# More ticks behind the gate columns, one reciprocal for both halves of a tile's numerators, and the last rows scaled by two engines

## The chip, the cores and the metric

One core of a Trainium2 chip runs the whole program. The metric is device microseconds of one execution; a kernel's time is the median of its runs. Five engines have a queue each and run their queues in order: TensorE (PE; its weight loads are listed as PEld), VectorE (DVE), ScalarE (ACT), GpSimd (POOL) and SyncE (SP, which here only issues DMAs).

## The reference

Three stages follow each other. B = 2, H = 8 heads, S = 576 tokens, D = 64, 128 features.

```python
# attention with positive features
q_p, k_p = phi(q_s), phi(k_s)                       # exp(projection - max)
kv  = np.einsum('bhsm,bhsd->bhmd', k_p, v);  z = np.sum(k_p, axis=2)
num = np.einsum('bhsm,bhmd->bhsd', q_p, kv)
den = np.einsum('bhsm,bhm->bhs', q_p, z)[..., None] + 1e-06
x = num / den                                       # as 1152 x 512
# a dense block
g = (x @ w1) * (x @ w2);  x2 = (g @ w3) @ w_out     # 512 -> 1024 -> 1024 -> 512
# a mixture of 8 experts, one expert for each token
logits = x2 @ w_gate;  expert_idx = np.argmax(logits, axis=1)
h = np.maximum(np.einsum('ecd,edf->ecf', disp, w1), 0.0)
y = np.einsum('ecf,efd->ecd', h, w2)
out[i] = gate_w[i] * y[expert_idx[i], pos[i]]       # kept tokens, zero for others
```

## The kernel before, in words

Each fp32 product is made of three TensorE passes over a high and a low half of both operands (`PASS`). ScalarE casts the high half; the low half is a subtraction on GpSimd or VectorE. The weights of the dense block come as 64-bit numbers: VectorE puts three operations (L325 to L327, or L350 to L355 for later ones) to a 128x512 piece to get an fp32, ScalarE casts, GpSimd subtracts (L331, L364).

The attention phase runs over nine tiles of 128 tokens. `num(i)` makes the numerators and denominators of a tile in two halves of four heads, one PSUM bank each from a pool of two (`pm`); VectorE adds EPS to the denominators (`dn`), takes reciprocals (`rd`) and multiplies (`x`). `x_tr` transposes the result to the operands `xh`, `xl`. In the last tiles TensorE also runs products of the dense block (`ab`, w = 0 into a `pm` bank, w = 1 into another pool's) as fill. Here a scheduler orders the queues of all engines but TensorE, whose order is that of the program.

Then a string, `PLAN`, lists products: `a` is a quarter of the rows of `x @ w1` and `x @ w2` for f, `W` is a row block of w3 @ w_out, `u` and `v` are the gate columns (`gate_t` transposes the raw W, `gate_u` multiplies it by w_gate), `l` the logits. From the mark `|` on every queue has the order of the program, and the preparation of weights is a list of tasks. `tick()` gives each active task one more step, at most one step for each engine: words on VectorE (two), cast on ScalarE, low half on GpSimd. The end of a step that frees a raw buffer issues the next load on SP. `need()` ticks until a task is done.

`END` is such a string for the rest: routing, and two rounds r0 and r1 over experts. A round gathers its tokens (`f`, `F`), transposes them (`t`, `T`: `r_pt`, `r_xc`), multiplies by W (`p`, `P`: `r_x2p`, `x2h`, `x2l`), makes the hidden layer (`h`, `H`: `r_hp`) with weights e1, and the result (`s`, `S`: `r_yt`, `r_py`) with e2; `scatter` scales rows by the gate (`yo`) and GpSimd writes them to `out` by an indirect DMA, three in a round. `.` is a tick, and `1` to `4` release the tasks of a round's e1 or e2, each of four loads of 512 KB cut in two pieces of 128x512 (`r1_e1_20` is piece 0 of load 2): ScalarE casts both, VectorE makes the low half of piece 0, GpSimd of piece 1, and GpSimd's frees the raw buffer. The raw buffers are two rings of two. `x` asks for r1's e1 loads, `y` for its e2 loads. A round's pieces have the same name in the profile with the round's digit left out (`r_e_20l`).

Of the kernel before, what the change touches and what calls it, by code (L numbers as in the profile page):

```python
# [8 lines left out]
F32 = mybir.dt.float32  # L9
# [5 lines left out]
ALU = mybir.AluOpType  # L15
AX = mybir.AxisListType.X

B, H, S, D, M = 2, 8, 576, 64, 128
NT = B * S
DM = H * D  # L20
# [3 lines left out]
G = 96  # L24
BIG = 1.0e6
SCALE = float(D) ** -0.25
EPS = 1e-6 * M
# [27 lines left out]

END = "l<kAkrArfAAArfw>AAAA>AA<At.ttLttMt>1K.p..K.p..Rp..p..p..RpF.2h..h.R.h..Fh..h..h..x3h..h..s.TT.sTT.sTT.s..ssy4P..P..P..P..P..P..P.H.H.H.H.H.HHHSSSS"


@with_exitstack
def attention_moe_kernel(ctx: ExitStack, tc: tile.TileContext, qT, kT, v, om, w1, w2, w3, wo, wg, e1, e2, cap, out):
    nc = tc.nc
    V = nc.vector
    A = nc.scalar

    const = ctx.enter_context(tc.tile_pool(name="const", bufs=1))
    sm = ctx.enter_context(tc.tile_pool(name="sm", bufs=1))
# [12 lines left out]
    def px(nm):  # L81
        return psx.tile([128, 512], F32, tag="px", name=nm)

    def u(shape, dt, nm):
        return unit.tile(shape, dt, tag="u", name=nm)

    def kq(shape, dt, nm):
        return kqp.tile(shape, dt, tag="kq", name=nm)
# [7 lines left out]
    def pm(nm):  # L96
        return psm.tile([128, 512], F32, tag="pm", name=nm)
# [14 lines left out]
    late, hold, leave = [False], [False], set()  # L112
# [9 lines left out]
    def pump():  # L122
        full = set()
        for t in todo:
            r = t["ring"]
            if r and t["raw"] is None and r not in full:
                if out_of[r] < LIM[r]:
                    out_of[r] += 1
                    t["raw"] = t["load"]()
                else:  # L130
                    full.add(r)

    def tick(n=1):
        for _ in range(0 if hold[0] else n):
            used = set()
            while todo and (todo[0]["key"][0][0] != "e" or todo[0]["key"][:2] in leave) and (todo[0]["ring"] is None or sum(t["ring"] is not None for t in active) < 2):
                active.append(todo.pop(0))
            for t in list(active):
                engs, fn, end = t["st"][0]
                if used & set(engs):  # L140
                    continue
                used |= set(engs)
                t["st"].pop(0)
                fn(t)
                if end:
                    out_of[t["ring"]] -= 1
                    pump()
                if not t["st"]:
                    active.remove(t)
                    done_of[t["key"]] = t["got"].get("r", True)  # L150
# [102 lines left out]

    def num(i):
        x = tmp.tile([128, H, D], F32, tag="x", name=f"x{i}", bufs=2)
        for g in range(2):
            ps = pm(f"nu{i}_{g}")
            for h in range(4):
                hh = 4 * g + h
                for t0 in (0, 64):  # L260
                    b = 0 if i < 4 or (i == 4 and t0 == 0) else 1
                    nc.tensor.matmul(out=ps[t0:t0 + 64, h * (D + 1):(h + 1) * (D + 1)], lhsT=qpT[i][:, hh, t0:t0 + 64],
                                     rhs=kvz[b][:, hh, :], start=True, stop=True)
            p4 = ps[:, 0:4 * (D + 1)].rearrange("p (h d) -> p h d", d=D + 1)
            dn = sm.tile([128, 4, 1], F32, tag="dn", name="dn", bufs=4)
            rd = sm.tile([128, 4, 1], F32, tag="rd", name="rd", bufs=4)
            V.tensor_scalar(out=dn, in0=p4[:, :, D:D + 1], scalar1=EPS, scalar2=None, op0=ALU.add)
            V.reciprocal(out=rd, in_=dn)
            V.tensor_tensor(out=x[:, 4 * g:4 * g + 4], in0=p4[:, :, 0:D], in1=rd.to_broadcast([128, 4, D]), op=ALU.mult)
        xs[i] = x  # L270

    def x_tr(i):
# [214 lines left out]
    def gate_t(f):  # L487

        raw = raws.pop(f)
        ps = px(f"wT{f}")  # L490
        for d in range(4):
            nc.tensor.transpose(out=ps[:, d * 128:(d + 1) * 128], in_=raw[:, d * 128:(d + 1) * 128], identity=ident)
        wT[f] = kq([128, 4, 128], F32, f"wT{f}")
        A.copy(out=wT[f], in_=ps.rearrange("p (d m) -> p d m", d=4))

    def gate_u(f):
        ps = px(f"u{f}")
        t = wT.pop(f)
        for d in range(4):
            nc.tensor.matmul(out=ps[:, 0:E], lhsT=t[:, d], rhs=wgT[:, d], start=(d == 0), stop=(d == 3))  # L500
        A.copy(out=u_all[:, f], in_=ps[:, 0:E])

    def logits(f, cs):
        for c in cs:
            nc.tensor.matmul(out=lgp[c * 32:c * 32 + E, 0:C], lhsT=u_all[:, f], rhs=g_t[f][:, c * C:(c + 1) * C],
                             start=(f == 0), stop=(f == 7))
        if late[0]:
            tick()
# [18 lines left out]
    for i in range(11):  # L527
        for st in STEP:
            if st in "Tt" and i < 9:
                q_tr(i, "Tt".index(st))  # L530
            if st in "Pp":
                phi_g(11 + i, "Pp".index(st))
            if st == "N" and 1 <= i < 10:
                num(i - 1)
            if st == "X" and 2 <= i:
                x_tr(i - 2)
            if st in "Aa" and i >= 7 and fill:
                ab_mm(*fill.pop(0))
        if i == 1:
            conv12(1)  # L540
# [38 lines left out]
    for p in PLAN.split():  # L579
# [10 lines left out]
        elif what == "u":  # L590
            gate_t(*arg)
        elif what == "v":
            gate_u(*arg)
        elif what == "o":
            conv_o(*arg)
        elif what == "t":
            conv3(*arg)
        elif what == "l":
            logits(*arg, range(4))
        elif what == "h":  # L600
            logits(*arg, range(2))
        elif what == "e":
            for w in range(2):
                ab_mm(*arg, w)
        elif what == "z":
            zeroed()
        elif what == "|":
            flush()
            late[0] = True
            mark()  # L610
        elif what == "g":

            wg_sb = kq([E, DM], F32, "wg_sb")
            nc.sync.dma_start(out=wg_sb, in_=wg)
            ps = px("wgT")
            for d in range(4):
                nc.tensor.transpose(out=ps[:, d * E:(d + 1) * E], in_=wg_sb[:, d * 128:(d + 1) * 128], identity=ident[:E, :E])
            A.copy(out=wgT, in_=ps[:, 0:4 * E].rearrange("p (d e) -> p d e", e=E))
# [248 lines left out]

    def scatter(nm, g, py, idx, gt):
        yo = u([G, DM], F32, f"{nm}_yo{g}")
        V.tensor_scalar(out=yo, in0=py[:G], scalar1=gt[:, g:g + 1], scalar2=None, op0=ALU.mult)  # L870
        nc.gpsimd.indirect_dma_start(out=out, out_offset=bass.IndirectOffsetOnAxis(ap=idx[:, g:g + 1], axis=0),  # L871
                                     in_=yo, in_offset=None, bounds_check=NT - 1, oob_is_err=False)

    def result(nm, wy, got):
        hh = got.pop("hh")
        for g in range(3):
            py = (pa, pm)[g % 2](f"{nm}_py{g}")
            for f in range(8):
                for s, r in PASS:
                    nc.tensor.matmul(out=py[:G], lhsT=hh[r][f // 4][:, f % 4, g * G:(g + 1) * G], rhs=wy[f][s],  # L880
                                     start=(f == 0 and (s, r) == (0, 0)), stop=(f == 7 and (s, r) == (1, 0)))
            scatter(nm, g, py, got["odx"], got["gt"])
            yield
# [76 lines left out]

    for p in END:
        if p == "A":
# [119 lines left out]
```

## Time and profile before

| | before |
|---|---|
| median of 3 runs | 344.31 us (343.56 to 346.01) |
| the profiled execution | 343.41 us, span 341.5 us |
| TensorE busy | 325.2 us, 95% |
| VectorE, ScalarE, GpSimd busy | 64%, 43%, 39% |
| TensorE's granted clock, mean | 0.994 |

The span is what the profile shows of one execution, from the first to the last instruction; the execution's own time is 1.9 us more. Busy time is summed over the span; the share of one stretch can be far from it. A wait is listed with the engine and line that ended it.

### The profile page before, as it was taken

Reading aid. Unit: us, or ns where it says so; the run is one execution under the profiler, and the core shown is the slowest. Engines: PE = TensorE matmul, PEld = TensorE weight load, DVE = VectorE, ACT = ScalarE, POOL = GpSimd, SP = SyncE. Lnnn points to the kernel's source line nnn. Section 1 sums busy time; section 2 is a strip of 40 time slices with the busy share of each in tenths; the row PEclk is TensorE's granted clock in tenths of the full one; section 3 lists DMA queues with packets and bytes.
Section 4 is the critical chain, followed back from the end, with each engine's and each line's share of the span. In section 5 each row is a group of like instructions: output and inputs, shape, how many; then the busy total and the mean of one; then the engine's idle time right before and its main releaser. Section 6 shows DMA issues by size and latency. Waiting matters only on the chain. (4 is left out here: it accounts for less than half of the span.)

```text
span 341.5 us, 7108 instructions
## 1 busy us (share of the span) xinstructions
PE 325.2 (95%) x2771; PEld 300.8 (88%) x2771; DVE 218.8 (64%) x426; ACT 146.4 (43%) x347; POOL 134.2 (39%) x118
## 2 busy tenths in 40 slices
PE   8999989999999999999998898999999998999991
PEld 6899889999998889898878786899899998999991
DVE  4979999999986864935394763281596766332110
ACT  4999899743321413324333332121462645332100
POOL 3737910333353324545336664014062562243021
PEclk9999999999999999999999999999999999999997
DMA  7995200344465728972335430893869791510011
GB/s 253 396 316 199 64 2 7 97 147 125 126 184 163 270 38 190 211 148 61 125 89 157 134 114 0 289 129 88 298 112 183 224 274 41 209 48 2 1 30 46
DMA packets 25147, 47.76 MB, mean 140 GB/s; under 512 B 3116, under 2 KB 12460, under 8 KB 25110
## 3 DMA queue, kind: packets, MB, share of 16 engines
q1 hardware_dynamic: 16950, 40.18, 39.0%
q10 hardware_dynamic: 7104, 3.54, 6.3%
q0 software_dynamic: 1056, 3.54, 3.8%
q8 instruction: 24, 0.39, 0.5%
q14 instruction: 13, 0.11, 0.1%
HBM read 38.98 MB, written 8.27 MB: 138 GB/s over the span
## 5 line engine op out<-in xcount | busy, mean ns | idle before, releaser
L433 PE MATMUL ab<-xh,w_hl 128*128 128x288 f32 x512 | 108.2, 299 | 4.8 <-POOL w_hl L364 3.8
L433 PEld LDWEIGHTS ab<-xh,w_hl 128*128 128x128 f32 x512 | 83.4, 188 | 8.1 <-POOL w_hl L364 4.5
L433 PE MATMUL ab<-xl,w_hl 128*128 128x288 f32 x256 | 75.5, 295 | 0.0
L433 PEld LDWEIGHTS ab<-xl,w_hl 128*128 128x128 f32 x256 | 48.1, 188 | 0.0
L472 PE MATMUL W<-wo_hl,w_hl 128*128 128x512 f32 x192 | 46.3, 397 | 0.0
L472 PEld LDWEIGHTS W<-wo_hl,w_hl 128*128 128x128 f32 x192 | 35.5, 188 | 8.2 <-issue 0.5
L350 DVE TENSOR_SCALAR w_f<-w_raw 128x512 uint32<-128x512 uint32 x22 | 17.4, 789 | 23.5 <-POOL w_hl L364 23.4
L364 POOL TENSOR_TENSOR w_hl<-w_f,w_hl 128x512 fp32r<-128x512 f32 x22 | 29.6, 1358 | 5.3 <-ACT w_hl L360 5.3
L405 DVE STREAM_TRANSPOSE gs<-g 128x576 f32<-128x576 f32 x16 | 19.5, 1221 | 13.5 <-POOL g L446 13.3
L836 PE MATMUL r_x2p<-r_xc,W 128*128 128x288 f32 x192 | 26.5, 297 | 0.0
L836 PEld LDWEIGHTS r_x2p<-r_xc,W 128*128 128x128 f32 x192 | 25.7, 188 | 0.1
L480 POOL TENSOR_TENSOR W<-W_raw,W 128x512 fp32r<-128x512 f32 x8 | 10.8, 1355 | 37.3 <-ACT W L479 19.2
L331 POOL TENSOR_TENSOR wo_hl<-wo_f,wo_hl 128x512 fp32r<-128x512 f32 x8 | 11.5, 1433 | 34.7 <-PE xT L276 18.4
L437 ACT COPY a_sb<-ab 128x288 f32<-128x288 f32 x32 | 12.7, 398 | 27.6 <-PE ab L433 27.6
L331 POOL TENSOR_TENSOR w_hl<-w_f,w_hl 128x512 fp32r<-128x512 f32 x10 | 14.0, 1402 | 22.4 <-ACT w_hl L330 22.4
L360 ACT CAST w_hl<-w_f 128x512 fp32r<-128x512 f32 x22 | 13.7, 625 | 18.8 <-DVE w_f L355 18.8
L446 POOL TENSOR_TENSOR g<-a_sb,b_sb 128x288 f32<-128x288 f32 x12 | 10.6, 879 | 25.0 <-ACT b_sb L445 25.0
L355 DVE SCALAR_TENSOR_TENSOR w_f<-w_raw,w_f 128x512 uint32<-128x512 uint32 x22 | 19.2, 872 | 0.6
L871 POOL DMA_INDIRECT out<-r_yo,r_odx x6 | 5.6, 932 | 34.4 <-DVE r_yo L870 22.6
L448 DVE TENSOR_TENSOR g<-a_sb,ab 128x288 f32<-128x288 f32 x20 | 8.9, 448 | 15.4 <-PE ab L433 15.4
L210 PE MATMUL pjq<-om_hl,q_hl 128*128 128x256 f32 x108 | 16.3, 293 | 0.0
L210 PE MATMUL pjk<-om_hl,k_hl 128*128 128x256 f32 x108 | 15.6, 297 | 0.6 <-ACT k_hl L198 0.5
(233 smaller groups left out, 693.3 us busy)
## 6 DMA issues: line engine op xcount, KB each, us to landing
w_raw<-in_w SPq DMA_DIRECT2D x32, 512.0 KB, 3.7
wo_raw<-in_wo SPq DMA_DIRECT2D x8, 512.0 KB, 3.5
gd<-gs ACTq DMA_DIRECT2D x12, 288.0 KB, 6.0
v<-in_v SPq DMA_DIRECT2D x9, 260.0 KB
k<-in_kT SPq DMA_DIRECT2D x9, 256.0 KB, 4.3
q<-in_qT SPq DMA_DIRECT2D x9, 256.0 KB, 6.6
out<-zero SPq DMA_DIRECT2D x1, 2304.0 KB, 9.7
r_e_0r<-in_e SPq DMA_DIRECT2D x4, 512.0 KB
```

Of the source, the lines that this page charges most:

```text
L210: nc.tensor.matmul(out=ps[:, r * 256:(r + 1) * 256], lhsT=t[:, s, k * 128:(k + 1) * 128], rhs=om_hl[:, w], start=(n == 0), stop=(n == 2))
L331: nc.gpsimd.tensor_tensor(out=hl[1], in0=f.bitcast(F32), in1=hl[0].bitcast(F32), op=ALU.subtract)
L350: V.tensor_scalar(out=f, in0=r[:, :, 1], scalar1=3, scalar2=0x3FFFFFF8, op0=ALU.logical_shift_left, op1=ALU.bitwise_and)
L355: V.scalar_tensor_tensor(out=t["f"], in0=r[:, :, 0], scalar=29, in1=t["f"], op0=ALU.logical_shift_right, op1=ALU.bitwise_or)
L360: A.copy(out=h[:, 0], in_=t["f"].bitcast(F32))
L364: nc.gpsimd.tensor_tensor(out=h[1], in0=t["f"].bitcast(F32), in1=h[0].bitcast(F32), op=ALU.subtract)
L405: V.transpose(out=sts[b][:, :, :, f % GF], in_=g_t[f][:, b * S:(b + 1) * S].rearrange("p (j t) -> p j t", t=32))
L433: nc.tensor.matmul(out=p[:, :C], lhsT=w12[f][w][s][:, k, :], rhs=xhl[c][r][:, k], start=(n == 0), stop=(n == 11))
L437: A.copy(out=abp[f, c], in_=p[:, :C])
L472: nc.tensor.matmul(out=p, lhsT=w3_t[f, k // 4][s][:, k % 4, :], rhs=wo_t[k][r], start=(n == 0), stop=(n == 23))
L480: nc.gpsimd.tensor_tensor(out=w_t[f][:, 1], in0=raw, in1=w_t[f][:, 0].bitcast(F32), op=ALU.subtract)
L836: nc.tensor.matmul(out=p4[d][:, :C], lhsT=w_t[f][:, s, d * 128:(d + 1) * 128], rhs=xc[r][f // 4][:, f % 4], start=(f == 0 and (s, r) == (0 ...
```

## The change

In `gate_t` and `gate_u` a tick is added behind ScalarE's copy, once the preparation runs as tasks. In `num`, the denominators of both halves go to one tile of eight, one reciprocal is taken of all, and both multiplies follow it; the tiles `dn` and `rd` have two buffers in place of four. In `scatter`, for the third group of rows, VectorE scales the first 256 columns and ScalarE the others. In `END`, `3` (the release of r1's e1 tasks) moves from the place where r1's loads are asked for to one behind the first result and two steps of r1's transposes, and one tick is added behind a later `TT`.

```diff
-END = "...h..h..x3h..h..s.TT.sTT.sTT.s..ssy4P..P..P..P..P..P..P.H...
+END = "...h..h..xh..h..s.TT.3sTT..sTT..s..ssy4P..P..P..P..P..P..P.H...
...
     def num(i):
         x = tmp.tile([128, H, D], F32, tag="x", name=f"x{i}", bufs=2)
+        dn = sm.tile([128, H, 1], F32, tag="dn", name="dn", bufs=2)
+        rd = sm.tile([128, H, 1], F32, tag="rd", name="rd", bufs=2)
+        p4 = []
         for g in range(2):
...
-            V.tensor_scalar(out=dn, in0=p4[:, :, D:D + 1], scalar1=EPS, scalar2=None, op0=ALU.add)
-            V.reciprocal(out=rd, in_=dn)
-            V.tensor_tensor(out=x[:, 4 * g:4 * g + 4], in0=p4[:, :, 0:D], in1=rd.to_broadcast([128, 4, D]), op=ALU.mult)
+            p4.append(ps[:, 0:4 * (D + 1)].rearrange("p (h d) -> p h d", d=D + 1))
+            V.tensor_scalar(out=dn[:, 4 * g:4 * g + 4], in0=p4[g][:, :, D:D + 1], scalar1=EPS, scalar2=None, op0=ALU.add)
+        V.reciprocal(out=rd, in_=dn)
+        for g in range(2):
+            V.tensor_tensor(out=x[:, 4 * g:4 * g + 4], in0=p4[g][:, :, 0:D], in1=rd[:, 4 * g:4 * g + 4].to_broadcast([128, 4, D]), op=ALU.mult)
...
     def gate_t(f):
...
         A.copy(out=wT[f], in_=ps.rearrange("p (d m) -> p d m", d=4))
+        if late[0]:
+            tick()
...
         A.copy(out=u_all[:, f], in_=ps[:, 0:E])
+        if late[0]:
+            tick()
...
     def scatter(nm, g, py, idx, gt):
         yo = u([G, DM], F32, f"{nm}_yo{g}")
-        V.tensor_scalar(out=yo, in0=py[:G], scalar1=gt[:, g:g + 1], scalar2=None, op0=ALU.mult)
+        n = DM // 2 if g == 2 else DM
+        V.tensor_scalar(out=yo[:, 0:n], in0=py[:G, 0:n], scalar1=gt[:, g:g + 1], scalar2=None, op0=ALU.mult)
+        if n < DM:
+            A.mul(out=yo[:, n:DM], in_=py[:G, n:DM], mul=gt[:, g:g + 1])
```

TensorE's and SP's queues keep their order. On VectorE, ScalarE and GpSimd it changes at many places; three follow. In each the rows are an engine's queue from top to bottom, first of the kernel before, then of the changed one.

GpSimd around the products of f = 5 in `PLAN`. `w1_5_hl` and `w2_5_hl` are the two weights of those products, `W5` the block that `W5` in `PLAN` makes. Before:

```order
L446 TENSOR_TENSOR g4_2205<-a_sb_2424,b_sb_2443 128x288
L364 TENSOR_TENSOR w1_5_hl_2458<-w1_5_f_2427,w1_5_hl_2458 128x512
L480 TENSOR_TENSOR W5_2501<-W5_raw_2502,W5_2501 128x512
L364 TENSOR_TENSOR w2_5_hl_2490<-w2_5_f_2472,w2_5_hl_2490 128x512
L446 TENSOR_TENSOR g5_2549<-a_sb_2529,b_sb_2550 128x288
L364 TENSOR_TENSOR w3_6_0_hl_2531<-w3_6_0_f_2492,w3_6_0_hl_2531 128x512
```

The same place on GpSimd in the changed kernel:

```order
L448 TENSOR_TENSOR g4_2182<-a_sb_2398,b_sb_2416 128x288
L366 TENSOR_TENSOR w1_5_hl_2427<-w1_5_f_2400,w1_5_hl_2427 128x512
L366 TENSOR_TENSOR w2_5_hl_2449<-w2_5_f_2429,w2_5_hl_2449 128x512
L482 TENSOR_TENSOR W5_2478<-W5_raw_2479,W5_2478 128x512
L366 TENSOR_TENSOR w3_6_0_hl_2483<-w3_6_0_f_2460,w3_6_0_hl_2483 128x512
L448 TENSOR_TENSOR g5_2531<-a_sb_2511,b_sb_2532 128x288
```

The low half of w2_5 moved ahead of W5's, and w3_6_0's ahead of a product of g5.

GpSimd around the three scatters of round 0 (`out_0`), with the low halves of r1's e1 and e2. Before:

```order
L756 TENSOR_TENSOR r1_e1_10l_3688<-r1_e1_1r_3661,r1_e1_10h_3687 128x512
L756 TENSOR_TENSOR r1_e1_20l_3724<-r1_e1_2r_3663,r1_e1_20h_3723 128x512
L756 TENSOR_TENSOR r1_e1_30l_3795<-r1_e1_3r_3665,r1_e1_30h_3794 128x512
L871 DMA out_0<-r0_yo0_3878,r0_odx_3066 1152x512
L871 DMA out_0<-r0_yo1_3883,r0_odx_3066 1152x512
L871 DMA out_0<-r0_yo2_3888,r0_odx_3066 1152x512
L756 TENSOR_TENSOR r1_e2_00l_3920<-r1_e2_0r_3893,r1_e2_00h_3919 128x512
```

The same place on GpSimd in the changed kernel:

```order
L762 TENSOR_TENSOR r1_e1_10l_3801<-r1_e1_1r_3634,r1_e1_10h_3800 128x512
L880 DMA out_0<-r0_yo0_3844,r0_odx_3039 1152x512
L880 DMA out_0<-r0_yo1_3849,r0_odx_3039 1152x512
L880 DMA out_0<-r0_yo2_3854,r0_odx_3039 1152x512
L762 TENSOR_TENSOR r1_e1_20l_3837<-r1_e1_2r_3636,r1_e1_20h_3836 128x512
L762 TENSOR_TENSOR r1_e1_30l_3886<-r1_e1_3r_3638,r1_e1_30h_3885 128x512
L762 TENSOR_TENSOR r1_e2_00l_3906<-r1_e2_0r_3860,r1_e2_00h_3905 128x512
```

The scatters moved ahead of the low halves of r1_e1's loads 2 and 3, whose raw buffers the loads r1_e2_2r and r1_e2_3r take.

VectorE around tile 8's numerators in the attention phase (`nu8_0` and `nu8_1` are its two banks; `wo2_f`, `w1_3_f` and the like are pieces of weights that it converts). Before:

```order
L326 SCALAR_TENSOR_TENSOR wo3_f_1601<-wo3_raw_1599,wo3_f_1601 128x512
L325 TENSOR_SCALAR wo0_f_1610<-wo0_raw_1608 128x512
L267 TENSOR_SCALAR dn_1393<-nu8_0_1384 128x4
L327 SCALAR_TENSOR_TENSOR wo3_f_1601<-wo3_raw_1599,wo3_f_1601 128x512
L268 RECIPROCAL rd_1394<-dn_1393 128x4
L267 TENSOR_SCALAR dn_1407<-nu8_1_1398 128x4
L269 TENSOR_TENSOR x8_1383<-nu8_0_1384,rd_1394 128x256
L268 RECIPROCAL rd_1408<-dn_1407 128x4
L326 SCALAR_TENSOR_TENSOR wo0_f_1610<-wo0_raw_1608,wo0_f_1610 128x512
L269 TENSOR_TENSOR x8_1383<-nu8_1_1398,rd_1408 128x256
```

The same place on VectorE in the changed kernel:

```order
L328 SCALAR_TENSOR_TENSOR wo2_f_1652<-wo2_raw_1650,wo2_f_1652 128x512
L268 TENSOR_SCALAR dn_1360<-nu8_0_1362 128x4
L329 SCALAR_TENSOR_TENSOR wo2_f_1652<-wo2_raw_1650,wo2_f_1652 128x512
L268 TENSOR_SCALAR dn_1360<-nu8_1_1372 128x4
L327 TENSOR_SCALAR w1_3_f_1779<-w1_3_raw_1777 128x512
L269 RECIPROCAL rd_1361<-dn_1360 128x8
L328 SCALAR_TENSOR_TENSOR w1_3_f_1779<-w1_3_raw_1777,w1_3_f_1779 128x512
L271 TENSOR_TENSOR x8_1359<-nu8_0_1362,rd_1361 128x256
L271 TENSOR_TENSOR x8_1359<-nu8_1_1372,rd_1361 128x256
```

Both multiplies moved behind the second half's denominators, and two conversions of w1_3 stand ahead of the first.

## Rows read from the trace of the kernel before

**Rows 1.** The page, part 1: busy time, share and instructions of each engine.

```profile
PE 325.2 (95%) x2771; PEld 300.8 (88%) x2771; DVE 218.8 (64%) x426; ACT 146.4 (43%) x347; POOL 134.2 (39%) x118
```

**Rows 2.** TensorE's waits: us in total, times, longest us.

```profile
PE ab L433 <- POOL w_hl L364: 3.8, 3, 1.5
...
PE ab L433 <- ACT a_sb L437: 0.8, 1, 0.8
```

**Rows 3.** Timeline of TensorE around 181 us: start, duration, instruction, idle before.

```profile
180.43 0.29 PE L433 MATMUL ab<-xl,w_hl 128*128 128x288 f32 x1
181.74 0.53 PE L433 MATMUL ab<-xh,w_hl 128*128 128x288 f32 x2 [1.02 <-POOL w_hl L364]
```

**Rows 4.** Timeline of TensorE, start of round 1's hidden layer.

```profile
305.51 0.30 PE L857 MATMUL r_hp<-r_x2h,r_e_00h 128*128 128x288 f32 x1
...
308.70 0.29 PE L857 MATMUL r_hp<-r_x2h,r_e_10h 128*128 128x288 f32 x1
```

**Rows 5.** Timeline of GpSimd around 180 us.

```profile
179.17 1.29 POOL L480 TENSOR_TENSOR W<-W_raw,W 128x512 fp32r<-128x512 f32 x1 [3.68 <-ACT u_all L501]
180.42 1.26 POOL L364 TENSOR_TENSOR w_hl<-w_f,w_hl 128x512 fp32r<-128x512 f32 x1
```

**Rows 6.** Timeline of ScalarE, VectorE and TensorE around 282 us.

```profile
281.19 0.62 ACT L752 CAST r_e_20h<-r_e_2r 128x512 fp32r<-128x512 f32 x1 [3.21 <-DMA r_e_2r<-in_e]
...
282.29 1.02 DVE L825 TENSOR_TENSOR r_xc<-r_pt,r_xc 128x384 fp32r<-128x384 f32 x2 [1.98 <-ACT r_xc L824]
...
282.90 1.22 PE L820 MATMUL r_pt<-ident,r_xg 96*128 96x96 f32 x8 [0.89 <-DVE r_xc L825]
```

**Rows 7.** Timeline of SP, VectorE and GpSimd, 291 to 305 us.

```profile
291.58 0.33 SPq L739 DMA_DIRECT2D r_e_3r<-in_e  x1
...
292.77 2.06 DVE L870 TENSOR_SCALAR r_yo<-r_py,r_gt 96x512 f32<-96x512 f32 x3 [2.41 <-issue]
...
293.80 0.97 POOL L871 DMA_INDIRECT out<-r_yo,r_odx  x1 [2.29 <-DVE r_yo L870]
300.67 0.95 POOL L871 DMA_INDIRECT out<-r_yo,r_odx  x1 [5.91 <-DVE r_e_20l L756]
304.22 0.92 POOL L871 DMA_INDIRECT out<-r_yo,r_odx  x1 [2.60 <-DVE r_x2l L840]
```

**Rows 8.** The page, part 6: DMA issues, count, size each, us to landing.

```profile
w_raw<-in_w SPq DMA_DIRECT2D x32, 512.0 KB, 3.7
```

**Rows 9.** Timeline of ScalarE, 301 to 304 us.

```profile
301.72 0.62 ACT L752 CAST r_e_31h<-r_e_3r 128x512 fp32r<-128x512 f32 x1
303.31 0.40 ACT L839 CAST r_x2h<-r_x2p 128x288 fp32r<-128x288 f32 x1 [0.96 <-PE r_x2p L836]
```

**Rows 10.** Timeline of VectorE around 276 us.

```profile
275.86 3.85 DVE L756 TENSOR_TENSOR r_e_00l<-r_e_0r,r_e_00h 128x512 fp32r<-128x512 f32 x1
```

**Rows 11.** Timeline of VectorE, 77 to 79.5 us.

```profile
77.54 0.68 DVE L326 SCALAR_TENSOR_TENSOR wo_f<-wo_raw,wo_f 128x512 uint32<-128x512 uint32 x1
78.14 0.40 DVE L325 TENSOR_SCALAR wo_f<-wo_raw 128x512 uint32<-128x512 uint32 x1
78.47 0.15 DVE L267 TENSOR_SCALAR dn<-nu 128x4 f32<-128x4 f32 x1
...
79.13 0.17 DVE L268 RECIPROCAL rd<-dn 128x4 f32<-128x4 f32 x1
79.21 0.14 DVE L267 TENSOR_SCALAR dn<-nu 128x4 f32<-128x4 f32 x1
```

**Rows 12.** Timeline of TensorE around 79 us.

```profile
79.06 0.43 PE L433 MATMUL ab<-xh,w_hl 128*128 128x288 f32 x2
...
79.46 0.82 PE L433 MATMUL ab<-xh,w_hl 128*128 128x288 f32 x2
```

**Rows 13.** Windows, core 0: stretch, length, busy PE, PEld, DVE, ACT, POOL, clock, DMA.

```profile
40.00:79.40 39.40, 37.84 (x506) 35.37 (x502) 37.91 (x101) 28.27 (x74) 9.51 (x8) 1.00 0.23 68
```

**Rows 14.** Timeline of VectorE, the end of the span.

```profile
334.58 0.75 DVE L870 TENSOR_SCALAR r_yo<-r_py,r_gt 96x512 f32<-96x512 f32 x1 [3.44 <-PE r_py L909]
```

## What the change does to the time: the prediction

> **What bounds the kernel now.** I read the page's busy times first. TensorE is busy 325.2 us of a span of 341.5, so the kernel is bound by one engine that hardly ever stops [rows 1]; what is left to win or lose is in its pauses, and any new wait of TensorE costs its full length. The second view is therefore the list of TensorE's waits. Its largest entry is 3.8 us in three pieces: the products `ab` wait for GpSimd, which makes the low half of a weight (`low`, L364). A wait of 0.8 us for ScalarE's `a_sb` is smaller [rows 2]. The third reading is the timeline around one of the three pieces, then around the places where the order of instructions moves.
>
> The profiled execution took 343.41 us: the span of 341.5 and 1.9 around it. The median of the three runs is 344.31, 0.9 above it. I add up changes on the trace and put the sum on the median.
>
> **Ticks behind the gate columns.** At 180.43 TensorE starts a matmul and its next one starts at 181.74, with 1.02 us idle [rows 3]. Matmuls of this shape follow each other every 0.133 us (24 of them between 305.51 and 308.70 [rows 4]), so 1.31 - 0.13 = 1.18 us are lost, 0.16 more than the idle time shown. GpSimd ran W5's low half at 179.17 and only then w2_5's, 180.42 to 181.68 [rows 5], which is the moment TensorE goes on. The other two pieces, before f=6 and f=7, have the same shape: `W6` and `W7` stand ahead of `w2_6` and `w2_7`. In the changed order GpSimd takes `w2_5`, `w2_6` and `w2_7` before the W of their number. Each low half then stands 1.3 us earlier by the swap alone (W's 1.29 us), and earlier still by the ticks ahead of it: with one more step of a task at each gate column, the conversion starts some 3 us sooner. I take all three stalls as gone: 3.8 + 3 x 0.16 = 4.3 us. Late next would be W's own low half, now behind; it is used only in the rounds, long after, so it costs nothing there. Bounds: -3.8 if the 0.16 is an artefact of modelled ends, -2 if one of the pieces half remains.
>
> **The release of round 1's weights, in the T stage.** Before, ScalarE waited 3.21 us for the load `r1_e1_2r` and began its cast at 281.19; the casts `r1_xc` behind it came late, VectorE's followed at 282.29 and TensorE's transposes at 282.90, 0.89 idle [rows 6]. With the release moved behind the first transposes no such cast stands there. Gain 0.9; at most 1.2, at least 0 if a later cast takes its place.
>
> **The same move, in round 1's products.** GpSimd now has the three scatters of round 0 ahead of `r1_e1_20l` and `r1_e1_30l`; before they were behind. A scatter waits until the one ahead of it has been written, since all go to `out`: they started at 293.80, 300.67 and 304.22, so 6.87 and 3.55 us apart, though VectorE had made all three `yo` by 294.83 [rows 7]. Queued behind the last one now: the two low halves, and behind these on SP the loads `r1_e2_2r` and `r1_e2_3r`, whose buffers they free; behind the loads on ScalarE the casts `r1_e2_20h`/`21h`, and behind those `r1_x2h` of d=2, which TensorE needs for the hidden layer. The chain in the time of before: the first scatter at 294.45 (VectorE makes one low half, about 0.65 us, ahead of `yo0`); the third two gaps of 3.55 later, 301.55; its issue to 302.5; the low half to 303.8; a load of 512 KB 3.7 us [rows 8], to 307.6; two casts of 0.62 that overlap a little, to 308.7; `x2h` of d=2, 0.40; two casts for the next load, `x2h` of d=3 from 310.0, ready at 310.4; the durations of both casts are in [rows 9]. TensorE comes to d=3 18 matmuls after the start of the hidden layer at 305.51 [rows 4], at 307.9. So it waits 2.5 us there, and loses another 0.4 since `yo0` holds the bank that the last `x2p` wants: 3.0. That is the case where both gaps are the short one. The long gap had loads of 512 KB in flight, three of them issued up to 291.58 [rows 7]; by the new order one, `r1_e2_1r`, should be. A third of the difference of 3.32 is 1.1, so I take 4.1. Bounds: 3.0, and 3.0 + 3.3 = 6.3 with the long gap again; below 3.0 only if a scatter doesn't wait for the one ahead of it, which is a rival. VectorE's halves of these conversions may come late as well: `r1_e1_00l` took 3.85 us where GpSimd worked back to back [rows 10]; I leave that in the bound.
>
> By the Trainium skill, "SBUF — State Buffer", section "Who interferes with whom", a VectorE instruction with two SBUF inputs and a GpSimd instruction that reads SBUF exclude each other, and the second to issue waits for all of the first. The row of 3.85 us agrees. By that rule alone the chain above would lengthen only where VectorE's half is the last one in, which would put the term nearer to 6.3 than to 4.1.
>
> **One reciprocal.** Nine reciprocals go, at 0.08 us of VectorE's time each (79.13 to 79.21 [rows 11]): 0.7 us. What the edit adds is a wait: the first half's `x` multiply now stands behind the second half's denominators, and its bank comes free later. With `ab` running in the fill, TensorE's next product takes that bank: the matmul at 79.46 shows 0.82 us for two, where the pair normally takes 0.43, so it is already the last one in [rows 12]. VectorE has no room here: busy 37.91 of 39.4 us from 40.0 to 79.4 [rows 13]. In the changed order its queue ahead of tile 8's first `x` holds two more of L325, five more of L326 and L327, and eight reciprocals fewer, counted over the whole queue to that place. By the starts of one to the next, L325 takes 0.33 (78.14 to 78.47) and the others 0.60 (77.54 to 78.14) [rows 11]: 0.7 + 3.0 - 0.7 = 3.0 us later. VectorE's idle 1.5 us of that stretch may take up half of it: 1.5. Conversions against GpSimd may be stretched, so between 1.5 and 3.0 I take 2.3. The same conversions are then done earlier for what follows, and the wait of 0.8 us for `a_sb` [rows 2], which stands behind a weight's cast, should vanish: 1.5 net. Bounds: -0.7, if TensorE never waits for it, to +3.0.
>
> The Trainium skill, "Perfetto Trace Analysis", section "Optimizing Scalar/DVE Operations", says that grouping into larger operations can raise throughput when the engine is saturated. VectorE is saturated here, so by that rule the edit gives its 0.7 us and the sum would be 2.2 lower. The count above speaks against it, since the wait for the second half is added.
>
> **The last rows.** VectorE's `yo` took 0.75 us, alone, with the last scatter behind it [rows 14]. Two halves on two engines: between 0.38 and 0.75; I take 0.42, a gain of 0.3. In round 0 this lies beside other work.
>
> **Sum:** -4.3 - 0.9 + 4.1 + 1.5 - 0.3 = +0.1, so 343.5 on the profiled execution and 344.4 on the median.
>
> **Rivals.** *The gains alone.* If a scatter doesn't hold the next one until it has been written, the low halves pass early and the hidden layer's 4.1 doesn't come: 344.4 - 4.1 = 340.3; without the numerators' 1.5 too, 338.8. For it: the trace names no DMA as releaser of the scatters. Against: the second started 5.91 us idle after `yo1` was there. *The slow scatters.* If the first scatter takes 6.87 again and the loads behind it stretch the others too, TensorE waits longer ahead of the hidden layer: 3.0 + 2 x 3.32 = 9.6, which is 344.4 + 5.5 = 349.9. With the first alone it is 346.6, and slower by over 1% from a stall of 7.5 us on. For it: other loads now fall into just this stretch. Against: by the order only one of them is in flight. *The grouped reciprocal pays.* VectorE gains 0.7, TensorE doesn't wait: 344.4 - 2.2 = 342.2. For it: a full VectorE; against: the rows of tile 8.
>
> **How the numbers follow.** 1% of 344.31 is 3.44 us, about what a measurement of this kernel can tell from no change. Forecast 0.45 and the grouped reciprocal 0.13 are both within 1%; gains alone 0.25, faster; slow scatters 0.17, slower. The lower end is at 340.0: the gains alone with the numerators' loss reach 340.3. The upper end is at 347.8: the long first gap (+2.2) with the numerators at 3.0 (+1.5) gives 348.1, a shade beyond.
>
> **What would show it.** In the trace after: no wait of `ab` for `w_hl` at f=5, 6, 7 (else the first term is wrong); no idle before the first `r1_pt`; TensorE idle 2.5 to 4 us in the first `r1_hp`, released by ScalarE's `r1_x2h`, with a cast that waits for a load ahead of it; `ab` matmuls of the fill waiting for `x`, 1 to 1.5 us at tiles 7 and 8 together; the last `yo` in two pieces side by side. The prediction fails if the scatters follow each other in about a microsecond, if the fill's waits stay at what they were, or if the wait ahead of the hidden layer is above 7.5.

## The result, and the profile after

| | before | after |
|---|---|---|
| median, first 13 runs each | 344.35 us | 348.14 us (345.63 to 352.12) |
| median, a second set (16 and 9 runs) | 343.96 us | 346.26 us |
| the profiled execution | 343.41 us, span 341.5 | 345.63 us, span 343.8 |
| ratio to before, 95% | | 1.0101 [1.0077, 1.0125] and 1.0076 [1.0053, 1.0100] |

The changed kernel is slower, by about 1% or a little less. 344.4 was forecast, with 347.8 as the upper end; the median of the first set is beyond it, that of the second is not. The ratios, and the means below, leave out three executions that took far longer than their sets: 352.12 us of the first set here, 805.54 of `fill` and 1765.04 of before.

TensorE's queue has the same order in both kernels, so the span can be cut at the same instructions and the two traces laid side by side. The table does so by start times of TensorE: of the first `tq`, the first `W`, the last `wT`, the long run of `r_x2p` in round 1, the first `r_hp` of round 1, its weights `e_10` and `e_20`, and the last matmul.

| stage, us | before | after | difference | forecast |
|---|---|---|---|---|
| to the first `tq` | 35.37 | 35.89 | +0.5 | 0 |
| attention, fill | 75.46 | 77.68 | +2.2 | +1.5 |
| `W` and `ab` of `PLAN` | 103.32 | 98.75 | -4.6 | -4.3 |
| to round 1's `x2p` | 78.49 | 77.16 | -1.3 | -0.9 |
| round 1's `x2p` | 12.87 | 13.31 | +0.4 | +0.4 |
| hidden layer, weights `e_00` | 3.19 | 6.71 | +3.5 | +3.7 |
| hidden layer, weights `e_10` | 3.19 | 4.61 | +1.4 | 0 |
| to the last matmul | 22.32 | 22.31 | 0 | 0 |
| to the end | 7.3 | 7.4 | +0.1 | -0.3 |

The list of TensorE's waits in the kernel after (total, times, longest) answers to [rows 2]:

```profile
PE ab L435 <- DVE x L271: 2.9, 3, 1.5
PE r_hp L863 <- ACT r_x2h L845: 2.2, 2, 2.0
PE pjk L210 <- DVE kp L215: 1.6, 1, 1.6
PE tq L226 <- ACT qpT L227: 1.4, 1, 1.4
```

The three waits for GpSimd's low half, 3.8 us, are gone, and so are `a_sb`'s 0.8 and the transposes' wait of [rows 6]. In their place stand waits for `x` and for `r_x2h`. The wait for `kp` is at 10 us, where the order is the same in both kernels; where it stands in other profiles here it is between 0.4 and 1.6, so it is no part of the change. The stage ahead of the first `tq` takes 35.4 to 36.3 us in the profiles here, with the change and without.

The chain of the new wait, from the timelines of the kernel after: GpSimd, SP, ScalarE, VectorE, then TensorE.

```profile
291.31 0.96 POOL L880 DMA_INDIRECT out<-r_yo,r_odx  x1 [2.91 <-DVE r_yo L877]
295.68 0.94 POOL L880 DMA_INDIRECT out<-r_yo,r_odx  x1 [3.40 <-DVE r_e_00l L762]
299.24 0.92 POOL L880 DMA_INDIRECT out<-r_yo,r_odx  x1 [2.61 <-ACT r_x2h L845]
300.18 1.30 POOL L762 TENSOR_TENSOR r_e_20l<-r_e_2r,r_e_20h 128x512 fp32r<-128x512 f32 x1
...
301.51 0.33 SPq L745 DMA_DIRECT2D r_e_2r<-in_e  x1
...
305.05 0.62 ACT L758 CAST r_e_20h<-r_e_2r 128x512 fp32r<-128x512 f32 x1 [6.46 <-SPq L1012]
305.57 0.61 ACT L758 CAST r_e_21h<-r_e_2r 128x512 fp32r<-128x512 f32 x1
306.09 0.39 ACT L845 CAST r_x2h<-r_x2p 128x288 fp32r<-128x288 f32 x1
...
306.51 0.46 DVE L846 TENSOR_TENSOR r_x2l<-r_x2p,r_x2h 128x288 fp32r<-128x288 f32 x1
...
306.53 0.40 PE L863 MATMUL r_hp<-r_x2h,r_e_00h 128*128 128x288 f32 x1 [1.99 <-ACT r_x2h L845]
307.02 0.40 PE L863 MATMUL r_hp<-r_x2l,r_e_00h 128*128 128x288 f32 x1
307.26 0.29 PE L863 MATMUL r_hp<-r_x2h,r_e_00l 128*128 128x288 f32 x1
...
309.98 0.44 PE L863 MATMUL r_hp<-r_x2h,r_e_10l 128*128 128x288 f32 x1
310.22 0.44 PE L863 MATMUL r_hp<-r_x2h,r_e_10h 128*128 128x288 f32 x1
```

The links from GpSimd to `x2h` are the forecast's: scatters 4.37 and 3.56 us apart [rows 7], the low half, a load of 3.5 us, two casts, `x2h`, TensorE idle. The idle time is 1.99 us ahead of d = 2 and 0.19 ahead of d = 3. Behind each of the two, the next matmuls start 0.49 and 0.24 us apart, since the second one needs `r_x2l`, which VectorE makes from `x2h`. That is some 0.5 us each time that the forecast has no term for, and with it the 2.2 us of idle time become most of the stage's 3.5. Nor has the forecast a word for the last two rows. Three microseconds behind the wait the matmuls start 0.24 us apart, where they took 0.133 [rows 4]. The windows of TensorE show why: length, busy time, granted clock, DMA share and GB/s.

```profile
300.00:305.00 5.00, 4.54 (x35) 1.00 0.62 201
305.00:310.00 5.00, 3.10 (x15) 0.93 0.13 52
310.00:315.00 5.00, 5.00 (x30) 0.73 0.01 3
315.00:320.00 5.00, 5.00 (x40) 1.00 0.00 0
```

The 0.07 and 0.27 that are missing in the two middle windows are 1.7 us of full clock, or 3.4 us at half of it: from 309.3 to 312.7 the granted clock was 0.50, that is 1.2 GHz in place of 2.4. It fell behind the wait, with TensorE busy again, and that is the 1.4 us of the weights `e_10`. In the second profile of the same kernel the stretch came earlier, from 307.9, with 0.79 and 0.87 in the two middle windows, and the stage of `e_10` took 3.81.

Each execution is listed with its span and its granted clock. (1 - clock) x span, called the clock part here, is then the time of the clock that was not granted. The stretch behind the last matmul is part of it and costs nothing; it is 0.9 to 2.4 us in the profiles, and all of the clock part where they show no other fall. The mean clock part is 2.2 us over the 29 runs of before that stand beside the first experiments, and 4.8 us over 12 of the first 13 of the changed kernel (2.0 and 3.8 in the second set). With this part taken off each run, the means are 342.4 and 343.0, and 341.9 and 342.6: 0.6 and 0.7 us apart. The forecast was 0.1. In five of the 12 runs the clock part is 5.9 to 7.7 us, more than 2.4 and one stretch of 1.7 can make. By this estimate their clock fell more than once, and since no profile shows a second fall, where it did stays open.

### The profile page after: what moved, and what is told of

It reads as the page before. It is cut to its first block, busy times and chain, and to the rows that moved or that the text cites. A ratio compares the mean times of both kernels' runs of the same rounds, so it can differ in the third digit from the quotient of the medians.

```text
span 343.8 us, 7094 instructions
## 1 busy us (share of the span) xinstructions
PE 326.5 (95%) x2771; PEld 302.4 (88%) x2771; DVE 211.5 (62%) x417; ACT 147.4 (43%) x349; POOL 135.1 (39%) x118
## 5 line engine op out<-in xcount | busy, mean ns | idle before, releaser
L352 DVE TENSOR_SCALAR w_f<-w_raw 128x512 uint32<-128x512 uint32 x22 | 15.5, 706 | 16.6 <-POOL w_hl L366 15.6
L357 DVE SCALAR_TENSOR_TENSOR w_f<-w_raw,w_f 128x512 uint32<-128x512 uint32 x22 | 21.1, 961 | 0.6
L448 POOL TENSOR_TENSOR g<-a_sb,b_sb 128x288 f32<-128x288 f32 x12 | 12.1, 1006 | 20.0 <-ACT b_sb L447 20.0
```

The source lines that it names most:

```text
L352: V.tensor_scalar(out=f, in0=r[:, :, 1], scalar1=3, scalar2=0x3FFFFFF8, op0=ALU.logical_shift_left, op1=ALU.bitwise_and)
L357: V.scalar_tensor_tensor(out=t["f"], in0=r[:, :, 0], scalar=29, in1=t["f"], op0=ALU.logical_shift_right, op1=ALU.bitwise_or)
L448: nc.gpsimd.tensor_tensor(out=g_t[f][:, c * C:(c + 1) * C], in0=abp.pop((f, c)), in1=b_sb, op=ALU.mult)
```

## The experiments

Theory A: the sum is about right and lacks TensorE's clock, which falls where TensorE stands still. Theory B: the clock has another cause or none of the change's, and the numerators cost far more than forecast. First the parts apart.

**ticks_only**: before, with the ticks alone.

```diff
     def gate_t(f):
...
+        if late[0]:
+            tick()
...
     def gate_u(f):
...
+        if late[0]:
+            tick()
```

> The kernel before with the added ticks in gate_t and gate_u alone. The first term of the sum: the three waits of ab for GpSimd's low half go, 4.3 us faster than before, 340.0. Rival: another engine is late next, and half of it comes, 342.

338.91 us against 344.37: ratio 0.9834 [0.979, 0.9879]. The stage of `PLAN` takes 98.75, as in the changed kernel, 4.6 less, and no other wait of `ab` takes the place of the three. One wait grows further on, that of round 1's transposes: 1.4 us in place of 0.9. The other 0.9 of the 5.5 is not found in the profile; a second set of runs (ticks_again, below) gives 4.5.

**num_back**: the changed kernel with the old numerators.

```diff
...
-        V.reciprocal(out=rd, in_=dn)
-        for g in range(2):
-            V.tensor_tensor(out=x[:, 4 * g:4 * g + 4], in0=p4[g][:, :, 0:D], ...)
...
+            V.reciprocal(out=rd, in_=dn)
+            V.tensor_tensor(out=x[:, 4 * g:4 * g + 4], in0=p4[:, :, 0:D], ...)
```

> The changed kernel with the old numerators (a reciprocal and a multiply for each half), all else kept. Theory A (what the result lost beyond the forecast is TensorE's clock: behind the wait of 2 us ahead of round 1's hidden layer the granted clock was 0.50 for 3.3 us in the changed kernel's trace): the waits of ab for x (2.9 us) go, the clock's fall stays, about 2.2 us faster than the changed kernel, 346. Theory B (the numerators' wait is the larger loss, and the profiled run shows its low end): 4 us or more faster, 344 or less, with the clock as in the changed kernel.

344.19, 3.9 below the first set of the changed kernel: close to theory B's figure, with the clock part at 4.0 us in place of 4.8. Without the clock part the means are 3.1 apart. The attention stage goes from 77.7 to 75.4. Theory B is right in that the numerators cost more than the 1.5 forecast.

**num_only**: before, with the new numerators alone (the same edit the other way round).

> The kernel before with the new numerators alone. In the changed kernel, undoing them gave 3.9 us in the median where the forecast had 1.5. Theory A (the wait of ab for x is all of it: about 2.9 us of waits in place of 0.3, and some of TensorE's clock behind the longest of them): 2.5 to 4 us slower than before, 347 to 348.4, with the same three waits of 0.9, 1.5 and 0.5 us at tiles 5, 7 and 8. Theory B (it costs more beside the ticks than alone, since the conversions that it brings forward relieve the wait for a_sb at 106 us here too): 1.5 us slower, 345.9.

347.91 against 343.96: ratio 1.0136 [1.0100, 1.0172], so it costs as much alone as beside the ticks. Waits of `ab` for `x`: 3.3 us, three, longest 2.0. The attention stage takes 78.08, 2.6 more. The clock part is 3.2 us against 2.0. Without it the means are 3.2 apart. Theory A's range holds. The profile has the wait of 1.95 us and no low stretch behind it or anywhere ahead of the last matmul, so where the clock fell in the other runs is not seen (a row of the timeline, then two windows of TensorE):

```profile
78.49 0.37 PE L435 MATMUL ab<-xh,w_hl 128*128 128x288 f32 x1 [1.95 <-DVE x L271]
...
75.00:80.00 5.00, 3.05 (x23) 1.00 0.47 129
80.00:85.00 5.00, 4.55 (x57) 1.00 0.49 156
```

Why more than 1.5? The timeline of VectorE after, ahead of tile 7's `x`, in which TensorE waits 1.53:

```profile
74.51 0.43 DVE L327 TENSOR_SCALAR wo_f<-wo_raw 128x512 uint32<-128x512 uint32 x1 [0.56 <-DMA wo_raw<-in_wo]
74.85 0.68 DVE L329 SCALAR_TENSOR_TENSOR wo_f<-wo_raw,wo_f 128x512 uint32<-128x512 uint32 x1
75.45 0.15 DVE L268 TENSOR_SCALAR dn<-nu 128x4 f32<-128x4 f32 x1
75.53 0.68 DVE L328 SCALAR_TENSOR_TENSOR wo_f<-wo_raw,wo_f 128x512 uint32<-128x512 uint32 x1
76.12 0.15 DVE L268 TENSOR_SCALAR dn<-nu 128x4 f32<-128x4 f32 x1
76.24 0.69 DVE L329 SCALAR_TENSOR_TENSOR wo_f<-wo_raw,wo_f 128x512 uint32<-128x512 uint32 x1
76.85 0.20 DVE L269 RECIPROCAL rd<-dn 128x8 f32<-128x8 f32 x1
76.96 0.51 DVE L289 TENSOR_TENSOR xl<-xT,xh 128x384 fp32r<-128x384 f32 x1
77.38 0.75 DVE L271 TENSOR_TENSOR x<-nu,rd 128x256 f32<-128x256 f32 x2
```

The conversions stand ahead of `x` as the order shows, and they wait themselves: they come earlier than their loads. The longest waits of VectorE from 40 to 82.9 us in the kernel after, neither of which stands in the kernel before:

```profile
DVE wo_f L327 <- DMA wo_raw<-in_wo: 1.6, 3, 0.6
DVE wo_f L327 <- POOL wo_hl L333: 1.3, 1, 1.3
```

The window of VectorE alone, in the kernel after (length, busy time, clock, DMA share, GB/s):

```profile
40.00:79.40 39.40, 35.36 (x93) 1.00 0.29 85
```

It was busy for 37.91 of these 39.4 us before [rows 13]. Its idle time did not take up half of the extra work; it grew from 1.5 to 4.0.

**low_first**: the changed kernel with four more ticks in `END` (the change itself had added two, one behind each of the last two `TT`), so that GpSimd has `r1_e1_20l` and `30l` ahead of the scatters.

```diff
-END = "...s.TT.3sTT..sTT..s..ssy4P...
+END = "...s.TT.3sTT..sTT....s....ssy4P...
```

> The changed kernel with four more ticks in END (two behind the last TT, two behind the last s), so that all four low halves of round 1's e1 stand ahead of the scatters on GpSimd again; the late release stays. Theory A: no wait ahead of the hidden layer, the clock stays at 1.00 there, 5 to 8 us faster than the changed kernel, 340 to 343. Theory B: only the wait itself goes, 2.2 to 3.3 us, 345 to 346. If the release itself, and not the place of the scatters, made the wait: no gain.

342.57, ratio 0.9947 [0.9916, 0.9978]: 5.5 below the changed kernel, more than the wait alone: the clock part falls from 4.8 to 2.7 us, and without it the means are 2.8 apart. The hidden layer takes 3.19 and 3.19 us again; the late release stays, and so does its gain in the stage ahead (77.16). So the wait came from the place of the scatters. In its timeline of GpSimd the profile names what a scatter waits for:

```profile
292.30 0.97 POOL L880 DMA_INDIRECT out<-r_yo,r_odx  x1 [0.16 <-issue]
299.16 0.95 POOL L880 DMA_INDIRECT out<-r_yo,r_odx  x1 [5.89 <-DMA out<-r_yo,r_odx]
302.72 0.92 POOL L880 DMA_INDIRECT out<-r_yo,r_odx  x1 [2.61 <-DMA out<-r_yo,r_odx]
```

**end_only**: before, with the new `END` alone.

> The kernel before with the new END alone. Theory A (the scatters ahead of the low halves: a wait of about 2 us and the clock behind it): 3.3 us of waits less the 0.9 of the T stage, and 2 us more of the clock, 4 to 5 us slower than before, 348.5 to 349.5, granted clock in the runs 0.985 in place of 0.995. Theory B (no clock loss from it): 2.4 slower, 346.8, clock 0.995.

346.92 against 343.96: ratio 1.0100 [1.0072, 1.0129]; theory B's figure, not A's. The weights `e_00` take 6.16, the transposes' stage 1.1 less. The clock part is 2.7 us against 2.0, and the median clock 0.992: something of it is there, far less than theory A had. The six runs stand apart: three at a clock of 0.993 or more took 346.18 to 346.27, three at 0.992 or less 347.56 to 348.56. The profile, one of the first three, shows the wait (1.55) and no low clock behind it, so the fall is not bound to come.

**fill**: the changed kernel, with TensorE kept busy in the wait.

```diff
     def hidden(nm, ev, got):
         x2 = got["x2"]
+        idle = px(f"{nm}_idle") if nm == "r1" else None
...
                 f, p = 2 * q + r2, p2[r2]
+                if nm == "r1" and (q, r2, k) == (0, 0, 2):
+                    for _ in range(20):
+                        nc.tensor.matmul(out=idle[:, :C], lhsT=w[0][:, 0, 0:128], rhs=x2[0][:, 0], start=True, stop=True)
```

> The changed kernel with 20 matmuls more (2.7 us) of 128x288 into a bank that nobody reads, on TensorE just where it waits ahead of the third k of round 1's hidden layer; they add to the work and leave nothing out. Theory A (the clock falls because TensorE stands still): granted clock 1.00 through the hidden layer, matmuls every 0.133 us again, 1.7 us faster than the changed kernel in its profile and 2 to 4 in the median, 344 to 346.4. If the clock falls for another cause: the low stretch stays, and the time is that of the changed kernel or up to 0.5 above.

347.0, 1.1 below the changed kernel's first set, and the weights `e_10` take 3.20 us: the clock stays up, 1.00 in the windows where it had been 0.93 and 0.73.

```profile
305.00:310.00 5.00, 4.88 (x36) 1.00 0.24 94
310.00:315.00 5.00, 5.00 (x40) 1.00 0.00 0
```

The clock part falls from 4.8 to 2.6 us. The median gains less than the 2 to 4 expected. Without the clock part the mean is 1.1 above the changed kernel's, which is what the 20 matmuls may take back; that is not measured by itself. So the mechanism was to be shown in a kernel where nothing else differs.

**low_first_num_back**: both losses undone.

> The changed kernel with the old numerators and with the four more ticks that put all low halves ahead of the scatters: the ticks, the late release and the halved last rows stay. If the two losses add: 348.1 - 3.9 - 5.6 = 338.6, at or below the ticks alone (338.9) by the 0.9 of the T stage and the 0.3 of the tail. If they share a cause (the clock), less than that: 340 to 341.

339.15 against 343.96: ratio 0.9864 [0.9839, 0.9888]; 0.55 above the plain sum. The two losses add, nearly.

**after_again**: the changed kernel once more.

> The changed kernel as it is, for a second profile. Theory A: granted clock of one half for some us behind the wait ahead of round 1's hidden layer, in stretches that differ from run to run (1 - clock, over all runs, 5.0 us of the span against 2.2 before). Theory B: the low clock stands elsewhere, behind the waits of the numerators at 76 us.

346.26, and the second profile told of above: the low clock stands behind the wait ahead of the hidden layer, not at 76 us.

**pause**: low_first_num_back with a wait of TensorE made by ScalarE, and no transfer, scatter or conversion moved.

```diff
             if f == 7:
+                if nm == "r1" and d == 2:
+                    for _ in range(20):
+                        spare = tmp.tile([128, C], F32, tag="a_sb", name="spare", bufs=3)
+                        A.copy(out=spare, in_=x2[0][:, 0].bitcast(F32))
                 A.copy(out=x2[0][:, d], in_=p4[d][:, :C])
```

> The kernel of low_first_num_back (which has no wait ahead of round 1's hidden layer) with 20 copies of 128x288 put on ScalarE ahead of x2h of d=2, about 6 us, so that TensorE stands still for some 2 us at the very place; no load, scatter or low half moves. Theory A (the standing still is enough for the clock to fall): the wait of about 2.2 us and behind it a granted clock of one half for some us, in most runs; 339.2 + 2.5 + 1.5 to 2.5 = 343 to 344, and 1 - clock over the span up from 2.1 us to 3.5 or more. Theory B (what lowers the clock is the traffic of the scatters and loads): the wait alone, 341.7, and 1 - clock stays at 2.1 us.

**pause_fill**: the same, with 16 matmuls in the wait, as in fill.

> The same with 16 matmuls (2.1 us) into a bank that nobody reads, on TensorE just where it would stand still. Theory A: the time of the pause without its clock part, 341.5 to 342, 1.5 to 2.5 below the pause alone, and 1 - clock near 2.1 us. Theory B: the same as the pause.

pause: 342.84, with a clock part of 2.6 us. pause_fill: 341.93, with a clock part of 1.6 us; that is 0.9 below pause, where theory A had 1.5 to 2.5.

The profile of pause has the wait, and of this execution no low clock:

```profile
304.76 0.40 PE L865 MATMUL r_hp<-r_x2h,r_e_00h 128*128 128x288 f32 x1 [2.09 <-ACT r_x2h L847]
...
306.82 0.29 PE L865 MATMUL r_hp<-r_x2h,r_e_10h 128*128 128x288 f32 x1
306.95 0.29 PE L865 MATMUL r_hp<-r_x2l,r_e_10h 128*128 128x288 f32 x1
```

Its 12 executions fall into two groups:

| | time, us | granted clock |
|---|---|---|
| pause, 5 of 12 | 341.20 to 341.66 | 0.993 to 0.998 |
| pause, 7 of 12 | 342.78 to 343.60 | 0.988 to 0.992 |
| pause_fill, 6 of 6 | 341.02 to 342.11 | 0.993 to 0.997 |

The same program, the same wait: where the clock stays up it costs 2.3 us over low_first_num_back (another set of runs; the stage took 2.7 more in the profiles), and where it falls 1.7 more (the means of the groups are 341.46 and 343.20). With TensorE kept busy the second group is gone. No profile of pause shows a fall in its place; that those of the second group stand behind the wait follows from pause_fill, and low_first_num_back, without the wait, has one run of five at 0.991. Theory A holds in its cause: standing still for 2 us can be enough, with no transfer moved. In its size it was too high, since the clock falls in a part of the executions only. The profiled one is one draw of them.

**old_tail_too**: low_first_num_back with the old scatter as well.

```diff
-        n = DM // 2 if g == 2 else DM
...
+        V.tensor_scalar(out=yo, in0=py[:G], scalar1=gt[:, g:g + 1], scalar2=None, op0=ALU.mult)
```

> The kernel of low_first_num_back with the old scatter (the last rows scaled by VectorE alone): ticks and late release only. Reading of the trace after: ScalarE's half of the last rows starts only when VectorE's has ended, so the split costs about 0.1 to 0.3; expected 0.1 to 0.3 below low_first_num_back, 338.9, with the stretch from TensorE's last matmul to the end back at 7.3 us. If the split gains 0.3 as forecast: 339.5.

**ticks_again**: the kernel of ticks_only, on the chip of old_tail_too.

> The kernel before with the added ticks alone, on the same chip as the kernel with ticks and late release. By the stages of the traces the late release with all low halves ahead of the scatters gives 1.7 in the transposes and takes 0.7 ahead of the hidden layer: ticks alone should be 0.5 to 1 slower than old_tail_too. If the two are equal, the late release is worth nothing here.

338.80 and 339.99 us, against 344.45 for before: ratios 0.9841 [0.9814, 0.9869] and 0.9868 [0.9839, 0.9897]. The first, ticks and late release with the low halves in front, is the fastest found, 1.6% below the kernel before; the lead on the ticks alone is 1.2 by the medians, where 0.5 to 1 was expected. A part of that has its place in the profile: ticks_again waits 1.65 us in round 1's transposes, and here too the clock falls behind it.

```profile
279.17 1.22 PE L824 MATMUL r_pt<-ident,r_xg 96*128 96x96 f32 x8 [1.65 <-DVE r_xc L829]
```

The window of TensorE just behind it:

```profile
280.00:285.00 5.00, 5.00 (x29) 0.66 0.00 0
```

For the tail, old_tail_too stands 0.35 below low_first_num_back, but in another set of runs, and the intervals of the two ratios overlap; the stretch behind the last matmul was 7.5 and not the 7.3 expected (7.7 in low_first_num_back). The timeline of the kernel after is plainer than either:

```profile
336.80 0.48 DVE L877 TENSOR_SCALAR r_yo<-r_py,r_gt 96x256 f32<-96x256 f32 x1 [3.38 <-PE r_py L918]
337.31 0.47 ACT L879 ACTIVATE r_yo<-r_py,r_gt 96x256 f32<-96x256 f32 x1 [13.01 <-DVE r_yo L877]
338.06 0.92 POOL L880 DMA_INDIRECT out<-r_yo,r_odx  x1 [3.45 <-ACTq L1012]
```

ScalarE's half starts when VectorE's has ended, and waits for it. The halves end 0.98 us after the first began, where one piece took 0.75 [rows 14].

## Why the prediction was wrong, point by point

The step that failed is the one on which the whole sum stands: "any new wait of TensorE costs its full length". The sum took every wait at its own length and had no term for TensorE's clock. Behind the new wait of 2 us TensorE ran at half its clock for 3.4 us in the profiled execution; that costs 1.4 there, and over all executions the clock part grew by 2.7 and 1.7 us in the mean of the two sets, behind this wait and wherever else it fell. No rival had it. The prediction does not use the granted clock of before at all; the row that could have raised the question was the spread of its three runs (343.56 to 346.01). In the 16 runs of before that stand beside the last experiments, the three with a clock below 0.991 took 345.64 to 347.10, the others 343.40 to 344.85.

A second step was mis-sized: the numerators, +1.5 in the sum, cost 3.1 to 3.2 without the clock (num_back, num_only). That the remainder still comes to 0.6 to 0.7 for 0.1 is in part luck. By the means without the clock part, the ticks gained 0.2 to 0.7 more than forecast, and the move of `3` with its tick cost 2.6 in place of 3.2 (end_only); this makes up for half or more of what the numerators cost too much.

The Trainium skill, "TensorE: Matmul & The Clock Gate", section "What's actually happening", says that activity releases a throttle, and that the point of a change shifts from run to run. The traces agree: with TensorE kept busy (pause_fill) the group with the lower clock is gone, and behind the same wait of the changed kernel the fall came at 309.3 in one profile and at 307.9 in the other.

*The ticks*: right, -4.6 for -4.3; without the late release they lengthen the transposes' wait (1.4 and 1.65 for 0.9). *The release in the T stage*: right, -1.1 to -1.4 for -0.9, in every kernel with the late release. *The scatters ahead of the low halves*: right in the chain up to `x2h`; in size, +3.9 for +4.1 without the clock, but partly by luck. The first gap was 4.37, between the two bounds as assumed. TensorE's idle time was 2.2 us in place of the 2.5 to 4 named as a sign, and stood ahead of d = 2 more than of d = 3; the waits for `r_x2l` behind it, which no term has, filled the sum. The +0.4 of the bank came as put down, though no row of before was given for it. VectorE's halves took 0.69 and 0.84 us here, so the stretching kept in the bound did not come. The rival of the gains alone falls: the scatters do wait for each other's writes. The slow scatters did not come.

*One reciprocal*: right in mechanism and sign, mis-sized, 2.2 to 2.6 by the stages for 1.5, and 3.9 by the medians, of which about 1 is clock; the 0.6 to 0.9 between are not found. The waits stand at tiles 5, 7 and 8 (0.87, 1.53 and 0.51 us), where the forecast had 1 to 1.5 at tiles 7 and 8 together and none at tile 5. Half of VectorE's idle time was to take up the extra work. The work brought forward met loads that had not landed and a buffer not yet free, and made 2.5 us of idle time more. The recovery at `a_sb`, 0.8, came. The rival that grouping pays falls with num_only.

*The last rows*: wrong in mechanism. Side by side was taken from the change's words. The halves run one after the other, and the path to the last scatter is 0.2 longer in place of 0.3 shorter. That is small, and the median can't tell it.

## What to carry to other kernels

A wait of the bounding engine has a second price where that engine is TensorE: look at the granted clock and the pace of the matmuls just behind the longest waits, in more than one execution, and put the possible fall into the range. When a change lets work run earlier, follow it back to its own loads and buffers before counting it as done earlier. A DMA that has to wait for another's write is a gate for everything behind it on its queue; put the short work that frees buffers ahead of it.

## What was not expected of the hardware

A standstill of 2.1 us let TensorE's clock fall in 7 of 12 executions of one program and left it up in the other five. In single profiles a fall came behind waits of 1.99 and 1.65 us (the two of the changed kernel) and of 1.65 (ticks_again); none came behind 1.95 (num_only), 1.72 (fill, in the attention stage), 1.60 (num_back) and 1.55 us (end_only). So the length of the wait alone does not tell, and what else decides is not shown here. The fall came after the work had started again (306.53 and 309.3 in the kernel after; 306.47 and 307.9 in its second profile; 279.17 and 280.9 in ticks_again), and lasted 3.4 us in the three profiles that have one.
